# The last batch's second deferred output block: stored at step 14 of chunk 4 in place of step 26 of chunk 3

## The chip, the cores and the metric

One core of a Trainium2 chip runs the program. The metric is the device time of one execution in microseconds (us), lower is better. "Before" is the kernel as it was, "after" the changed one. A trace has its own clock, which starts with the span.

## The reference, cut to what matters

```python
# u, v: (8, 3008, 256); z: (8, 3008, 64); w_in: (256, 2048); w_out: (2048, 256)
scores = (z @ z.T) / 3008                  # batch by batch
x = u * (np.maximum(scores, 0.0) ** 2 @ v)
h = x @ w_in
out = (h / (1 + np.exp(-1.702 * h))) @ w_out
```

The eight batches are independent. The kernel goes through a batch in six chunks of rows (0 to 5), five of 512 and a last one of 448. A score tile is squared on ScalarE and VectorE; because the scores are symmetric, a tile is computed once and its mirror image is made by a transposing DMA into a tile called `tt` (`ad` and `al` are two further kinds of tile that such DMAs fill, for the diagonal and for the last rows).

## The kernel before

The parts that the change and the argument touch. `attend` yields the TensorE steps of one chunk. In each step TensorE multiplies one block of the squared scores with `V`, and other work is slipped in between the steps by their number:

```python
for i in range(NCH):                                  # chunks 0..5
    # ...
    for n, step in enumerate(attend(b, i, b == 0 and i == 0)):
        # ...
        if i == 3 and n in (3, 26) and LAST2:         # <- the line that changes
            LAST2.pop(0)()                            # store one deferred block
        if (i, n) in load:
            load_u(b, load[i, n])
        # ...
        take(host, sched[i].get(n, 0))                # next score tile(s): matmul, square, transpose
        # ...
        step()
```

`LAST2` holds the stores of the last two output blocks of the batch before, put off so that they do not crowd the end of that batch. A store is one 32x32-block transpose on VectorE and then DMAs on SP's queue, four for the block concerned here:

```python
def store(b, k):
    # ...
    yo = pw.tile([P, CH // QW, QW, NCC], F32, name="yo", tag="yo", bufs=1)
    dve.transpose(yo[...], Y[b, k][...])              # cut
    # ...
    for cb in range(P // QW):                         # 4 pieces
        for r, t, n_ in parts:
            sp.dma_start(out[r:r + n_]..., yo[...])   # cut
```

The transposing DMAs of the squared tiles go out on the same queue:

```python
def turn_unit(b, i, jp, a):
    # ...
    sp.dma_start_transpose(TT[b, i, cj][...], a...)   # cut
```

The score pairs of a chunk are made one chunk ahead of their use. In the last batch the fourth tile of chunk 4 is made at step 34 of chunk 3. I call its transpose the **late transpose**; TensorE reads it at step 20 of chunk 4, right after four matmuls on an `ad` tile. The transpose of a `tt` tile issued last before it is its **neighbour**.

## Time and profile before

| | before |
|---|---|
| median of the first three runs | 1180.64 us (1180.33 to 1181.52) |
| profiled execution | 1180.15 us, span 1178.3 us, clock 0.999 |
| TensorE busy | 1171.0 us, 99% of the span |
| VectorE, ScalarE busy | 871.0 us (74%), 849.4 us (72%) |
| share of the DMA engines by queue | SP 52.8%, GpSimd 21.5% |

TensorE is the bound: whatever leaves its idle time alone leaves the time alone. A view of waits names, for an engine, what ended its idle time; a chain of waits follows the last instruction back to what released it. The lines are in the prediction.

### The profile page before, as it was taken

The numbers are of one execution on the slowest core, as the hardware profiler recorded it, in microseconds if no ns is written. First come the engines' busy times: TensorE is split into PE (matmuls) and PEld (weight loads), VectorE is DVE, ScalarE is ACT, GpSimd is POOL, SyncE is SP. The second block draws the span as 40 slices with busy tenths as digits, with TensorE's granted clock in tenths as the row PEclk, the third lists the DMA queues.
The fourth block names the chain that finished last, engine by engine and source line by source line (L and its number), as shares of the span: only waits on it lengthen the run. The fifth ranks groups of instructions, "written<-read, shape, count | busy, mean of one in ns | idle before, by whom it ended". The sixth has DMA issues, their size and how long they took to land.

```text
span 1178.3 us, 23585 instructions
## 1 busy us (share of the span) xinstructions
PE 1171.0 (99%) x9284; PEld 670.0 (57%) x9284; DVE 871.0 (74%) x1455; ACT 849.4 (72%) x1033; POOL 209.4 (18%) x294
## 2 busy tenths in 40 slices
PE   9999999999999999999999999999999999999998
PEld 3546764466644675446754467544674456744566
DVE  7789875878767786587865878658786587764776
ACT  7888874688647886478864787647877578772785
POOL 3033101231012310143101420024100241001000
PEclk9999999999999999999999999999999999999999
DMA  9998679766798677976779568895678955696023
GB/s 223 210 134 129 130 119 158 90 108 135 119 150 94 108 141 127 144 101 93 146 117 154 101 93 149 137 150 88 100 126 142 142 105 94 122 166 120 1 37 73
DMA packets 459039, 143.65 MB, mean 122 GB/s; under 512 B 424624, under 2 KB 453040, under 8 KB 458928
## 3 DMA queue, kind: packets, MB, share of 16 engines
q1 hardware_dynamic: 402464, 102.36, 52.8%
q0 software_dynamic: 55104, 38.49, 21.5%
q8 instruction: 72, 1.18, 0.4%
q10 hardware_dynamic: 1360, 1.31, 0.4%
q14 instruction: 39, 0.32, 0.1%
HBM read 60.29 MB, written 24.64 MB: 72 GB/s over the span
## 4 chain that ended last, share of the span: by engine, by line
PE 98%; ACT 1%; DMA 0%; issue 0%; SPq 0%; DVE 0%
PE o L367 40%; PE hg L408 28%; PE st L532 23%; PE sc L235 6%; PE st L535 1%; PE yp L506 1%; ACT rl L256 0%; DMA tt<-a 0%; PE w L99 0%; ACT W L452 0%; SPq L599 0%; ACT ZT L143 0%; ACT gf L416 0%; PE zp L135 0%; DVE a L270 0%
## 5 line engine op out<-in xcount | busy, mean ns | idle before, releaser
L416 ACT ACTIVATE gf<-hg 128x1024 f32<-128x1024 f32 (+1 forms) x384 | 385.3, 1004 | 114.6 <-PE hg L408 97.7
L256 ACT ACTIVATE rl<-sc 128x1024 f16<-128x1024 f32 (+1 forms) x301 | 287.4, 993 | 143.5 <-PE sc L235 98.4
L367 PEld LDWEIGHTS <-V 64*128 64x128 f16 (+1 forms) x4098 | 219.7, 94 | 252.5 <-issue 9.4
L408 PE MATMUL hg<-xt,W 128*128 128x512 f16 (+1 forms) x1408 | 354.6, 374 | 0.2
L367 PE MATMUL o<-a,V 64*128 64x512 f16 (+3 forms) x2278 | 296.1, 368 | 0.3 <-DVE a L270 0.3
L420 DVE TENSOR_SCALAR gt<-gf 128x1024 f16<-128x1024 f32 (+1 forms) x288 | 200.1, 695 | 114.2 <-ACT gf L416 113.1
L270 DVE TENSOR_TENSOR a<-rl 128x1024 f16<-128x1024 f16 (+1 forms) x266 | 178.1, 674 | 110.4 <-ACT rl L256 109.6
L195 POOL DMA_DIRECT2D uq<-in_u_dram x168 | 111.7, 673 | 739.9 <-PE sc L235 537.1
L367 PE MATMUL o<-tt,V 64*128 64x512 f16 (+1 forms) x1518 | 232.5, 377 | 1.0 <-DMA tt<-a 0.9
L408 PEld LDWEIGHTS <-W 128*128 128x128 f16 x1536 | 149.4, 98 | 125.6 <-issue 2.6
L532 PEld LDWEIGHTS <-WT 128*128 128x128 f16 x1472 | 139.1, 98 | 45.1
L532 PEld LDWEIGHTS <-W 128*128 128x128 f16 x1104 | 104.7, 98 | 32.2
L235 PE MATMUL sc<-ZT 64*128 64x512 f16 (+3 forms) x688 | 115.5, 356 | 0.6 <-ACT ZT L143 0.3
L418 ACT ACTIVATE gt<-gf 128x1024 f16<-128x1024 f32 (+1 forms) x96 | 98.9, 1030 | 3.1
L549 ACT ACTIVATE y<-st 128x256 f32<-128x256 f32 x192 | 70.6, 368 | 35.6 <-PE st L532 29.0
L532 PE MATMUL st<-gt,WT 128*128 128x256 f16 (+1 forms) x736 | 91.9, 268 | 0.0
L532 PE MATMUL st<-s,WT 128*128 128x256 f16 (+1 forms) x736 | 90.8, 268 | 0.0
L532 PE MATMUL st<-gt,W 128*128 128x256 f16 (+1 forms) x736 | 90.8, 268 | 0.0
L553 DVE SCALAR_TENSOR_TENSOR y<-st,y 128x256 f32<-128x256 f32 (+1 forms) x144 | 57.7, 408 | 24.5 <-ACT y L549 11.5
L384 DVE TENSOR_TENSOR xt<-o,ut 128x512 f16<-128x512 f32 x80 | 51.4, 683 | 28.5 <-PE o L367 28.5
L486 DVE TENSOR_TENSOR s<-s,gt 128x1024 f16<-128x1024 f16 (+1 forms) x96 | 65.0, 678 | 1.1
L484 DVE TENSOR_TENSOR s<-gt 128x1024 f16<-128x1024 f16 (+1 forms) x96 | 65.4, 681 | 0.0
(59 smaller groups left out, 670.9 us busy)
## 6 DMA issues: line engine op xcount, KB each, us to landing
out_dram<-yo SPq DMA_DIRECT2D x156, 128.0 KB, 2.8
uq<-in_u_dram POOLq DMA_DIRECT2D x140, 128.0 KB, 3.3
V<-in_v_dram POOLq DMA_DIRECT2D x35, 256.0 KB, 6.1
tt<-a SPq DMA_TRANSPOSE x232, 3.5
uq<-in_u_dram POOLq DMA_DIRECT2D x28, 112.0 KB, 4.7
out_dram<-yo SPq DMA_DIRECT2D x28, 96.0 KB, 6.4
uq<-in_u_dram SPq DMA_DIRECT2D x20, 128.0 KB, 4.3
wst<-in_moe_w_in_dram POOLq DMA_DIRECT2D x4, 512.0 KB, 6.0
```

The lines of the kernel that those rows point to most:

```text
L195: eng.dma_start(uq[k * QW:(k + 1) * QW, :n // QW].rearrange("t q c k -> t q (c k)"), src[:, :, cs])
L235: pe.matmul(sc[:, r, :q1 - q0], zt[h, 2 * kp + r, :], zt[h].rearrange("d n p -> d (n p)")[:, q0:q1], start=True, stop=True,)
L256: act.activation(rl[:, :, :n], sc[:, :, :n], AF.Relu, scale=csc)
L270: dve.tensor_tensor(a[:, :, :n], rl[:, :, :n], rl[:, :, :n], ALU.mult)
L367: ins = pe.matmul(acc[c][:, :n], V16[b][h, j].rearrange("p (c k) -> p k c", k=NCC)[:, c], weights(b, i, j)[h], start=(k, m) == first[c], s ...
L408: pe.matmul(hg[:, e, :n], W1[:, c, ff * P:(ff + 1) * P], XT[b, i][:, c, :n], start=(c == 0), stop=(c == NCC - 1),)
L416: act.activation(gf[:, :, :n], hg[:, :, :n], AF.Gelu_apprx_sigmoid, scale=1.0 / FSC)
L418: act.activation(g, gf[:, :, :n], AF.Copy, scale=FSC)
L420: dve.tensor_scalar(g, gf[:, :, :n], FSC, None, ALU.mult)
L484: dve.tensor_tensor(s_, a21, a22, ALU.add)
L532: pe.matmul(bank, right[:, ff], lhs()[:, f], start=first, stop=last, skip_group_check=True)
L549: act.activation(y[:, c, :, o], bank, AF.Copy, scale=1.0 / FSC)
```

## The change

The intent is to get the second deferred store of the last batch out of the way of the transposes issued late in chunk 3. `more` is true for all batches but the last, so the other batches keep their order.

```diff
-                if i == 3 and n in (3, 26) and LAST2:
+                if (i, n) in ((3, 3), (3, 26) if more else (4, 14)) and LAST2:
                     LAST2.pop(0)()
```

## The prediction

> **What bounds the kernel now.** I read the page first (busy shares, slices, the chain that ended last), then the waits of TensorE, then the chain and the timeline of the only place that the diff touches, which is the last of eight batches. The page:
>
> ```profile
> PE 1171.0 (99%) x9284; PEld 670.0 (57%) x9284; DVE 871.0 (74%) x1455; ACT 849.4 (72%) x1033; POOL 209.4 (18%) x294
> PE   9999999999999999999999999999999999999998
> PE 98%; ACT 1%; DMA 0%; issue 0%; SPq 0%; DVE 0%
> ```
>
> TensorE is busy 1171.0 of 1178.3 us, and the chain lies on it for 98% of the span. So only TensorE's own idle time can be won here, 7.3 us in all, most of it at the start and after the last matmul. Who TensorE waited for, over the whole span:
>
> ```profile
> PE w L99 <- DVE nil L75: 1.2, 1, 1.2
> PE o L367 <- DMA tt<-a: 0.9, 1, 0.9
> PE o L367 <- DVE a L270: 0.3, 1, 0.3
> ```
>
> In the middle of the kernel a single named wait is worth anything: 0.9 us, once, on a transposing DMA. The waits of the other kind of TensorE instruction, the weight loads, show the same event as 1.4 us, once, because the loads run ahead of the matmuls. The chain between 1072 and 1081 us shows what it was, with a view cut to that window:
>
> ```profile
> 1072.23 0.93 ACT rl L256
> ...
> 1073.18 0.63 DVE a L270
> 1073.80 0.14 DVE a L273
> 1073.95 0.07 SPq L599
> ...
> 1074.07 0.57 SPq L599
> ...
> 1075.24 0.47 SPq L599
> ...
> 1075.83 4.57 DMA tt<-a
> 1080.39 0.04 issue
> 1080.44 1.04 PE o L367 x8
> ```
>
> Read it backwards. Matmuls at 1080.44 waited for the transpose, which took 4.57 us from issue to landing. Its input was ready at 1073.94, but the DMA queue of SP was then issuing the four pieces of the second deferred output block (line 599), and only at 1075.83 did it come to the transpose. That block is the one that the diff moves. The timelines of SP and TensorE:
>
> ```profile
> 1071.92 1.23 SPq L298 DMA_TRANSPOSE tt<-a  x1
> 1073.24 2.47 SPq L599 DMA_DIRECT2D out_dram<-yo  x4
> 1075.83 1.25 SPq L298 DMA_TRANSPOSE tt<-a  x1
> 1077.44 2.98 SPq L277 DMA_TRANSPOSE al<-a  x2
> ```
>
> ```profile
> 1078.90 0.59 PE L367 MATMUL o<-ad,V 64*128 64x512 f16 x4
> 1080.44 1.04 PE L367 MATMUL o<-tt,V 64*128 64x512 f16 x8 [0.94 <-DMA tt<-a]
> ```
>
> **What the Trainium skill says.** "DMA: Bandwidth & Descriptors", section "Anatomy of one DMA — SWDGE (gpsimd) path", says that any semaphore wait happens on the issuing sequencer before dispatch; so an instruction behind another one on SP waits for it. The trace agrees: 1.89 us pass between input ready (1073.94) and issue (1075.83), filled by line 599. The same page, section "Queues, rings and completion order", says that each DMA engine consumes one row's descriptors in ring order, so the transpose also stands behind the stores' 384 KB as data. The trace agrees in kind: the transpose issued at 1071.92 ahead of the stores and the one at 1075.83 behind them are both among the slow ones, 4.7 and 4.57 us to landing, where the median of all 232 is 3.5. "Perfetto Trace Analysis", section "Summary: the profiler window per engine type", says that the window of such a DMA leaves out the data movement; hence I use the times to landing (4.57), not the 1.25 us of the timeline row.
>
> **The change, part by part.** Nothing is added or removed. For the last batch, one store moves from step 26 of chunk 3 to step 14 of chunk 4. The instruction lists of the two programs differ so: TensorE, ScalarE and GpSimd keep their order; on VectorE the layout transpose of the block (128x768, 0.97 us at 1071.81) moves behind the squares of three score tiles and the two gates; on SP the four stores move behind the late transpose and behind the two al transposes.
>
> *Removed on the path.* The late transpose is issued when its input is ready. Its producer does not get earlier: ScalarE's row at 1072.23 waits for the score matmul at 1071.83, so VectorE is done at 1073.94 as before. With 0.08 us to issue (1073.95 to 1074.02 in the chain) it goes out at about 1074.0. Landing: median 3.5 gives 1077.5; the slow 4.7 of its neighbour gives 1078.7. TensorE's weight loads need it when the loads before it end, 1075.26 + 3.74 = 1079.0, and the matmuls at 1078.90 + 0.59 = 1079.5. So it lands 0.3 to 1.5 us early for the loads and 0.8 to 2.0 us early for the matmuls. The whole 0.94 us goes.
>
> *Moved on VectorE.* The 0.97 us now falls at about 1077.4, after the square that ends at 1077.37. VectorE then has nothing until 1082.17 (the profile shows 4.81 us of idle there), so it costs nothing.
>
> *Moved on SP.* The four stores go out after the al transposes, from about 1080.4, taking 2.5 us; landing 2.8 more, so about 1086. SP's next own DMA is a store past 1125 us. On GpSimd's queue the last load of u (issued from 1082.27) shares the DMA engines with them; it is used by VectorE at 1092.45, over 5 us after it would land even if it took twice its 2.8 us. The al transposes are used by matmuls at 1086.57, and land by about 1082.4 as before or sooner.
>
> *Does the gain reach the end?* From 1081 to 1087 us TensorE is busy 5.97 of 6.00, and then 23.00 of 23.00 and 55.00 of 55.00 us up to 1165; the chain from there on is matmuls, one VectorE add and the last store. No other engine holds TensorE there, so everything shifts forward by the same amount. Sum: -0.94 + 0 + 0 = -0.94 us, 1180.64 - 0.94 = 1179.7 us, a change of 0.08%.
>
> **Rivals.** (1) *The wait shrinks but stays.* The transpose still shares the engines with the u load that GpSimd issued at 1070.34 to 1072.92 and stands behind the transpose of 1071.92. For: that neighbour took 4.7 us, and the slowest of all took 10.2. Against: without 384 KB of stores between the two, the queue has little left when the neighbour lands at 1076.6, and back-to-back transposes are issued 1.3 us apart elsewhere and land 3.2 to 3.8 us after issue. A landing of 6 us would leave 0.5 us of the wait: 1180.2 us. (2) *The stores do harm in their new place*, by delaying the u load of the last chunk or the al transposes. For: VectorE needs that load for its gate of chunk 5. Against: 5 us of slack or more for each, and SP issues the al pair first. Were there 1 us of delay, the time would be 1180.7, as before. (3) *Removing a wait uncovers another*: a score tile or gate not ready 0.94 us sooner. For: TensorE would reach chunk 5 sooner. Against: no other named TensorE wait exists past 1081 us, and the gates, scores and first up-products are themselves triggered by TensorE and shift with it. A new hitch would be 0.3 us or less: 1180.0. (4) *The gain is real but not visible in the medians*, as the three runs of before lie 1.19 us apart (1180.33 to 1181.52), more than the gain itself.
>
> **Range and chances.** I give 75% to the full gain, 15% to a part of it, 10% to nothing or to a small loss. All of these lie within 1 us; the spread of three runs and of chips adds about as much. So 1179.7 us, 1178.8 to 1180.8 in 8 of 10 cases. A 2% change would be 23.6 us, 25 times the only wait that is touched: within 2% is as good as certain, 0.98, with 0.01 on either side for a disturbed run.
>
> **What would show each step right or wrong.** In the profile of the changed kernel: the wait of the matmuls of o on tt is missing from TensorE's list; the transpose of tt of chunk 4 goes out at about 1074.0, right after the one of 1071.92, and lands by 1078.7; SP's four stores of the 96 KB kind stand behind the al pair near 1080.4; TensorE is busy 2.00 of the 2.00 us from 1079 to 1081; the span falls from 1178.3 to about 1177.4. I would be wrong if that transpose landed after 1079.5, if a new wait of TensorE past 1081 us appeared (on u's layout transpose or on al), or if the span fell by clearly more than 0.94 us, which would mean that idle time which I took for unconnected was hanging on it.

## More of the kernel before

Products of `x` with `w_in` are made in what the kernel calls up-groups.

One more line of the page matters later. It is from the list of DMA queues, with packets, megabytes and share of 16 engines' span:

```profile
q8 instruction: 72, 1.18, 0.4%
```

These are 72 packets, 1.18 MB together and some 16 KB each, on a queue of its own.

## The result, and the profile after

| | before | after |
|---|---|---|
| median | 1180.49 us (6 runs, 1180.13 to 1183.37) | 1179.29 us (6 runs, 1179.20 to 1179.84) |
| profiled span | 1178.3 us | 1177.7 us |
| TensorE's wait on `tt` | 0.9 us, once | none |

A ratio here is the mean time of one kernel's runs over the mean of the other's in the same rounds, so it is not quite the ratio of the medians quoted. It is 0.9986, with a 95% interval of 0.9973 to 0.9999: the same within 2%, and in the predicted range of 1178.8 to 1180.8 us.

The page of after, by busy time and by the engines of the chain that ended last:

```profile
PE 1171.1 (99%) x9284; PEld 670.1 (57%) x9284; DVE 870.9 (74%) x1455; ACT 849.7 (72%) x1033; POOL 208.0 (18%) x294
PE 99%; ACT 1%; DVE 0%; issue 0%
```

The work is that of before; the DMA and SP entries have left the chain. TensorE's waits in after, whole list (total us, times, longest):

```profile
PE w L99 <- DVE nil L75: 1.2, 1, 1.2
PE o L367 <- DVE a L270: 0.3, 1, 0.3
PE sc L235 <- ACT ZT L143: 0.3, 1, 0.3
PE zp L135 <- DVE zst L128: 0.2, 1, 0.2
PE sc L235 <- ACT rl L256: 0.2, 1, 0.2
```

The wait on `tt` is gone, and those that are left all fall in the first 15 us. SP's queue in after, as a timeline (start, us, instruction):

```profile
1072.42 3.28 SPq L298 DMA_TRANSPOSE tt<-a  x2
1077.93 2.69 SPq L277 DMA_TRANSPOSE al<-a  x2
1080.74 2.08 SPq L599 DMA_DIRECT2D out_dram<-yo  x4
```

The neighbour and the late transpose now go out one behind the other, the second at 1074.47, which is 0.03 us after its input is ready (VectorE ends at 1074.44). The DMA view of after, cut to the tenth of a microsecond in which the late transpose is issued (count, us to landing):

```profile
tt<-a SPq DMA_TRANSPOSE x1, 3.3
```

It lands at about 1077.8, 3.3 us after its issue. In before it took 4.57 us, from an issue 1.89 us after the input was ready. TensorE in after:

```profile
1079.40 0.59 PE L367 MATMUL o<-ad,V 64*128 64x512 f16 x4
1079.84 1.03 PE L367 MATMUL o<-tt,V 64*128 64x512 f16 x8
```

The transpose is there 2.0 us before its first matmul (1079.84 - 1077.8); these 2.0 us are its slack.

**The stall cost 1.10 us, not the 0.94 us that the profile prints as idle.** From the start of the four `ad` matmuls to the start of the first `tt` matmul it is 1080.44 - 1078.90 = 1.54 us before and 1079.84 - 1079.40 = 0.44 us after. The difference is 1.10. The printed idle time begins at the modelled end of the last `ad` matmul, and that end lies 0.16 us later than the next matmul would have started. The Trainium skill says in "Perfetto Trace Analysis", section "Tensor Engine Instruction (MATMUL, LD_WEIGHTS)", that this end is estimated; here the effect has a size.

**The spans differ by only 0.6 us because the profiled run of after lost 0.5 us at its start.** A TensorE line of the first 10 us, before:

```profile
8.56 0.39 PE L135 MATMUL zp<-ident,zst 128*128 128x128 f16 x4
```

and after:

```profile
9.05 0.40 PE L135 MATMUL zp<-ident,zst 128*128 128x128 f16 x4 [0.23 <-DVE zst L128]
```

The diff does not reach the first batch. The 0.49 us stays: the matmul on `sc` that begins chunk 4 starts at 1075.26 before and at 1075.76 after. Taking it off, 1.10 - 0.50 = 0.60, the difference of the spans.

### The profile page after: what moved, and what is told of

Same layout as the page of the kernel before. It is cut to its first block, busy times and chain, and to the rows that moved or that the text cites. A ratio compares the mean times of both kernels' runs of the same rounds, so it can differ in the third digit from the quotient of the medians.

```text
span 1177.7 us, 23588 instructions
## 1 busy us (share of the span) xinstructions
PE 1171.1 (99%) x9284; PEld 670.1 (57%) x9284; DVE 870.9 (74%) x1455; ACT 849.7 (72%) x1033; POOL 208.0 (18%) x294
## 4 chain that ended last, share of the span: by engine, by line
PE 99%; ACT 1%; DVE 0%; issue 0%
PE o L367 40%; PE hg L408 28%; PE st L532 23%; PE sc L235 6%; PE st L535 1%; PE yp L506 1%; PE w L99 0%; ACT rl L256 0%; ACT W L452 0%; ACT gf L416 0%; PE zp L135 0%; ACT ZT L143 0%; DVE a L270 0%; DVE zst L128 0%; DVE y L553 0%
```

## The experiments

The changed kernel once more and eleven variants ran, five times or more each, beside runs of before on the same chip. A microsecond is less than 0.1% of the time, and single executions of one kernel lie over 5 us apart at the most, so the traces carry the verdicts and the medians only support them: by their ratios all twelve are the same within 2%, and only the interval of e3 (1.0011 to 1.0035) lies clear of 1. A trace is one execution of its kernel. Other executions may lose more or less: single runs of e8 and e13 took 1179.34 and 1179.40 us, as little as the changed kernel. In the table, "lost" is the time from the start of the last `ad` matmul to that of the first `tt` matmul, less the 0.21 us that it takes in every trace without a wait; before has 1.11 us by this count. "Flight" is issue to landing of the late transpose.

| run | what is ahead of or beside the late transpose | flight, us | lost, us | median less that of before, us |
|---|---|---|---|---|
| (before) | 4 stores ahead on SP | 4.57 | 1.11 | |
| a0_after | nothing | 4.06 | 0 | 1179.69 - 1180.77 = -1.08 |
| e1_turn_stays | nothing (VectorE as before) | 3.44 | 0 | 1179.29 - 1180.77 = -1.48 |
| e2_gpsimd_queue | 4 stores beside it, GpSimd's queue | 7.06 | 1.74 | 1181.38 - 1180.77 = +0.61 |
| e3_eight_pieces | 8 half stores ahead on SP | 3.21 | 3.07 | 1183.06 - 1180.77 = +2.29 |
| e8_act_queue | 4 stores beside it, ScalarE's queue | 7.32 | 2.00 | 1180.97 - 1180.56 = +0.41 |
| e6_after_square | nothing; 4 stores right behind on SP | 3.37 | 0 | 1179.53 - 1180.56 = -1.03 |
| e9_twelfth_bytes | 4 stores of 8 KB ahead on SP | 4.88 | 1.07 | 1180.38 - 1180.56 = -0.18 |
| e4_three_stay | 3 stores ahead on SP | 4.78 | 0.80 | 1181.19 - 1180.56 = +0.63 |
| e10_before_96_more | 4 stores ahead on SP | 3.35 | 0.59 | 1180.56 - 1180.72 = -0.16 |
| e12_before_256_more | 4 stores ahead on SP | 4.59 | 1.13 | 1181.68 - 1180.72 = +0.96 |
| e11_after_32_more | nothing | 5.04 | 0 | 1179.61 - 1180.72 = -1.11 |
| e13_before_200_more | 4 stores ahead on SP | 4.53 | 1.32 | 1180.07 - 1180.58 = -0.51 |

One sum ties the rows together. In after, an unhindered first `tt` matmul starts 5.40 us after the transpose's input is ready (1079.84 - 1074.44), and some 0.05 us pass between landing and matmul. So what is lost is the lateness of the issue plus the flight less 5.35 us: 1.89 + 4.57 - 5.35 = 1.11 before, 5.22 + 3.21 - 5.35 = 3.08 in e3 (issue at 1079.75, input ready at 1074.53), and the other rows come out within 0.03 us. With the flight of after, 3.34 us, the late issue of before would have lost nothing (1.89 + 3.34 = 5.23): by this sum the stall of before needed both the late issue and the longer flight. No run has exactly this pair, so it is worked out, not shown.

The theory: the four stores, issued on SP ahead of the late transpose, make it late. The rivals: VectorE's moved transpose is what counts; the data in the DMA engines is, not SP's issue; and, later, something else on the DMA engines.

### The changed kernel again (a0_after)

No edit. 

> The changed kernel once more, paired with the kernel before. If the stall costs what the first matmuls of the late transpose lose from start to start (16.46 us before and 15.36 us after, from the first matmul of chunk 3 to the first matmul that needs the transpose), it is 1.1 us faster; if it costs only the idle time that the profile prints (0.94 us), 0.94 us. No TensorE wait on tt in the trace. The start of the kernel (first 10 us) differs by up to half a microsecond between runs of either kernel, which says nothing of the change.

The late transpose took 4.06 us and still landed 1.3 us early (1083.41, first use 1084.72): no wait on `tt`. The median is 1.08 us lower, but the ratio is 0.9996 (0.9983 to 1.0009), because one of six runs took 1184.43 us. That run is the profiled one, and its trace says why: in the first batch VectorE's layout transpose of `u` waited 4.7 us for its load, and TensorE then stood still for 3.3 us at 66 us, in code that the change does not touch.

### VectorE's part undone (e1_turn_stays)

```diff
         for cb in range(P // QW):
+            if b == B - 2 and k == NCH - 1:                # shortened: `piece` is the sp.dma_start of one piece
+                OFF.append(lambda cb=cb: piece(cb, sp))
+                continue
# ... and in the loop over the steps, the pop at (3, 26) kept as it was:
+                if (i, n) == (4, 14):
+                    while OFF:
+                        OFF.pop(0)()
```

> Only the four DMA stores move to chunk 4, the block's 0.97 us layout transpose on VectorE stays at step 26 of chunk 3. If SP's queue is the cause: no TensorE wait on tt, the late transpose is issued 0.1 us after its input is ready, time as the changed kernel (1.1 us below before). If VectorE's place in the order is the cause: the wait of 0.9 us stays and the time is that of before.

There is no wait on `tt`, and the median is 1.48 us below before. Only SP's part of the change is needed; in this trace VectorE's part is worth nothing.

### The stores on another queue (e2_gpsimd_queue, e8_act_queue)

```diff
-                OFF.append(lambda cb=cb: piece(cb, sp))      # of the kernel above, run at (4, 14)
+                OFF.append(lambda cb=cb: piece(cb, pool))    # e2: run at (3, 45); e8: act, run at (3, 35)
```

> The four stores of the block keep their time (about 1073 to 1076 us) but are issued by GpSimd after its u load, so SP is free and the data still shares the 16 DMA engines. If the delay is SP's issue alone: the late transpose goes out at about 1074.0 and lands within 3.5 us, no TensorE wait, 1.1 us below before. If the 384 KB of data are the cause: it goes out at 1074.0 but lands 5.5 us or more later, and a wait of 0.3 us or more stays.

> As the GpSimd experiment, but the four stores are issued by ScalarE's queue right after the late square (about 1073.2 us), where ScalarE has 2.5 us without work. SP is free, the 384 KB cross the DMA engines at the old time on another ring. If any data in flight beside the transpose delays it: issued at about 1074.0, landing after 5.3 us or more, a TensorE wait of 0.2 us or more stays. If the 7.06 us of the GpSimd experiment were special to GpSimd's queue: it lands within 4.5 us, no wait on tt, 1.1 us below before.

SP was free and issued the late transpose as soon as its input was ready; it landed later than before all the same. The chain of waits of the GpSimd kernel:

```profile
1073.80 0.15 DVE a L273
1073.95 0.02 issue
1073.97 7.06 DMA tt<-a
1081.03 0.05 issue
1081.08 1.04 PE o L367 x8
```

and of the ScalarE kernel:

```profile
1074.41 7.32 DMA tt<-a
```

The neighbour was slowed as well, from 4.7 to 6.0 and 6.3 us. So SP's issue time is not the only thing that can cause the stall: the transpose flew longer with the stores on another queue beside it than with the same stores ahead of it in its own (7.06 and 7.32 against 4.57 us). A packet on the queue q8 was in flight with the late transpose in all three (the section on the instruction fetch says what it is), but it began only at 1078.99 in e2 and 1079.56 in e8, when the transpose had flown 5.0 and 5.2 us already, so it is not the whole of it. In e8 it may be the last part: fifteen of the sixteen landing events had come by 1080.43, the sixteenth at 1081.73. The Trainium skill, "DMA: Bandwidth & Descriptors", section "Issuing engines are not separate DMA queues", says that DMAs from all issuing engines share the 16 DMA engines and interleave; the longer flights fit that, and show the cost. Why it is this large I did not find out.

### The stores right behind the late transpose (e6_after_square)

```diff
-                if i == 3 and n in (3, 26) and LAST2:
+                if (i, n) in ((3, 3), (3, 26) if more else (3, 36)) and LAST2:
```

> The second block is stored at step 36 of chunk 3, directly behind the late transpose on SP: only the order of two neighbours on SP is swapped against before, the bytes are in flight almost at the same time. If the order in the SP ring is what counts: the transpose lands within 3.5 us of 1074.0, no TensorE wait on tt, 1.1 us below before. If bytes in flight at that time delay it whatever the order: it lands after 5.3 us or more and a wait stays.

SP's queue:

```profile
1073.87 3.28 SPq L298 DMA_TRANSPOSE tt<-a  x2
1077.24 2.21 SPq L599 DMA_DIRECT2D out_dram<-yo  x4
```

The flight is 3.37 us, nothing is lost, and the median is 1.03 us below before. The whole gain comes from putting the late transpose ahead of the four stores; moving them a further 25 steps on is not needed. (Its profiled run, 1180.99 us, again had a hitch in the first batch, a 2.0 us wait of TensorE on ScalarE's cast of the weights.)

### More issue time, the same bytes (e3_eight_pieces)

```diff
+        if b == B - 2 and k == NCH - 1:
+            parts = [(r0, 0, n // 2), (r0 + n // 2, n // 2, n // 2)]
```

> As before, but in the last batch this block is stored in eight pieces of half the size: the same bytes, about twice the issue time on SP (some 4 us in place of 2.5). If SP's issue sets the end of the wait: the transpose goes out about 1.5 to 2 us later and TensorE's wait grows from 0.94 us by as much, so 1.5 to 2 us slower than before. If the data does: the landing stays at about 1080.4 us and the time is that of before.

SP was busy with the eight pieces for 5.50 us in place of 2.47, and 3.07 us were lost, 1.96 more than before; the median rose by 2.29 us. The transpose that goes out behind all 384 KB flies only 3.21 us. Time on SP ahead of the transpose therefore reaches the end of the kernel once the slack is gone.

### The same issue, almost no bytes (e9_twelfth_bytes)

Its output is wrong, which doesn't matter for the time. Each store writes 32 of 384 rows.

```diff
+        if b == B - 2 and k == NCH - 1:
+            parts = [(r0, 0, QW)]
```

> Wrong on purpose: the four stores stay at step 26 of chunk 3 on SP, but each writes only the first 32 of 384 rows (8 KB in place of 96), so most of that block of the output is not written. SP's issue time stays (about 2 us), the data is all but gone. If issue alone is enough for the stall: a TensorE wait near 0.9 us stays. If issue and data together are needed (1.8 us of issue delay against 2.0 us of slack): the transpose goes out near 1075.5 and lands 3.3 us later at about 1078.8, no wait, 1.1 us below before.

I had leant to the second of these, and it fell. SP's queue:

```profile
1073.31 2.11 SPq L601 DMA_DIRECT2D out_dram<-yo  x4
1075.54 1.24 SPq L298 DMA_TRANSPOSE tt<-a  x1
```

and the step of the chain of waits that follows:

```profile
1075.54 4.88 DMA tt<-a
```

32 KB in place of 384 KB ahead of it, and the late transpose still flew 4.88 us, and 1.07 us were lost. So it is not the bytes of the stores that make the flight of before 1.2 us longer than that of after. e3 above, and e10 below (3.35 us), say the same from the other side: behind all the bytes the flight can be as short as in after.

### A quarter of the stores moved (e4_three_stay)

```diff
-            if b == B - 2 and k == NCH - 1:                # of e1_turn_stays: put off to (4, 14)
+            if b == B - 2 and k == NCH - 1 and cb >= 3:    # the fourth piece alone
```

> Three of the four stores stay at step 26 of chunk 3, one moves to step 14 of chunk 4. The transpose goes out 0.57 us earlier than before (about 1075.25) behind 288 KB in place of 384, and lands some 0.9 us earlier, at about 1079.4, against a need at 1079.34: a wait of 0 to 0.3 us, so nearly the whole gain, 0.8 to 1.1 us below before. If the gain came in proportion to the stores moved, it would be a quarter, 0.3 us, and a wait of 0.7 us would stay.

The issue came 0.5 us earlier against the input than before (1.37 us late, not 1.89), as expected, but the flight of 4.78 us ate it up: 0.80 us were lost, close to the proportional rival's 0.7. The trace's landing events tell more. It has sixteen for this transpose. Fifteen had come by 1079.93, a flight of 3.2 us and early enough to lose nothing; the sixteenth came at 1081.50. In the packet records, a packet of 16 KB on the queue q8 had begun at 1079.51 and taken 0.96 us.

### Moving the instruction fetch (e10, e12, e11, e13)

That queue is the fetch of TensorE's program. The Trainium skill, "Runtime: NRT & Kernel Launch", section "Instruction fetch mechanics", says that an engine's instructions are fetched in blocks of 16 KiB (256 instructions) by a DMA queue of the sequencer. The trace agrees: 9284 matmuls and as many weight loads, 18568 instructions, make 72.5 such blocks against 72 packets, and between two of these packets lie 256 traced TensorE instructions on average. In before one began at 1077.56, took 1.17 us, and 21 packets of the transposes beside it took 1.27 to 1.62 us in place of some 0.02. In after the fetch began at 1078.06, just after the late transpose had landed.

More rows in TensorE's program shift the place of the fetch. Some up-groups of batch 5 compute 512 columns as twice 256, with the same results and next to no time:

```diff
+                if b == 5 and 8 <= q < 8 + GROUPS:   # 12, 32, 4, 25 groups: 96, 256, 32, 200 rows
+                    for m in range(2):
+                        x = slice(m * CH // 2, (m + 1) * CH // 2)
+                        pe.matmul(hg[:, e, x], W1[...], XT[b, i][:, c, x], ...)
+                    continue
```

> The kernel before, stores where they were; in batch 5 twelve up-groups compute each 512 columns as two of 256, which adds 96 rows to TensorE's program and next to no time. TensorE's program is fetched in pieces of 16 KB, one for each 256 rows, and one such fetch (1077.56 us before, 1.17 us on one DMA engine) met the late transpose. The rows move that fetch some 5 us earlier. If the fetch is needed for the stall: the transpose still goes out 1.9 us late behind the stores, but lands 3.2 to 3.4 us later, before it is needed: no wait on tt, about 1.0 us below before (less what the extra matmuls cost, at most 0.5 us). If the stores ahead of it suffice: landing after 4.5 us and a wait near 0.9 us as before.

> Control for the last one: 32 up-groups split, 256 more rows, so a whole fetch more and the fetches stand where they stood against the late transpose. If the fetch is needed for the stall: the wait on tt is back (0.5 to 1.2 us). If the extra rows themselves took the wait away: no wait on tt.

> The changed kernel with 32 more rows in TensorE's program, so that the fetch comes about 1.7 us earlier, while the late transpose moves its data (it landed 0.25 us before the fetch in the first profile of the changed kernel). If a fetch delays a transpose: it lands 4 to 5 us after issue in place of 3.3; with 2.0 us of slack before it is needed, still no wait on tt, and the time of the changed kernel. If the fetch does nothing: landing 3.3 us as before.

> The experiment with 96 rows moved the fetch onto the transpose before, which held up SP. With 200 more rows (25 groups split) and the stores still where the kernel before has them, one fetch should come some 11 us before the old place and the next about 3 us after it, 1080.6 us on the clock of before, clear of both transposes. If the fetch is needed for the stall: the late transpose goes out 1.9 us after its input is ready, lands 3.3 us later (1079.1 on the clock of before, need 1079.34), wait 0 to 0.1 us. If the stores ahead of it suffice: the wait of 0.9 us is back.

With 96 rows the fetch came about 5 us earlier on before's clock, as intended, and the late transpose flew 3.35 us. But 0.59 us were still lost: the fetch now met the neighbour, which flew 5.72 us and held SP for 2.32 us in place of 1.23, so the late transpose went out later. With 256 rows, a whole block, the fetch was back on the late transpose, and so were the flight of 4.59 us and 1.13 us lost. With 32 rows in the changed kernel the fetch fell on both transposes. The DMA view of that run at the issue of the late one:

```profile
tt<-a SPq DMA_TRANSPOSE x1, 5.0
```

It landed at 1079.00, 0.34 us before its first matmul at 1079.34: 1.7 of the 2.0 us of slack were used up and nothing was lost. So far the fetch explains the longer flights on SP's queue: 4.06 to 5.04 us in the six traces in which it was in flight with the late transpose for 0.7 us or more (before, a0, e4, e9, e11, e12), 3.21 to 3.44 in the other five (after, e1, e3, e6, e10).

The 200 rows put an end to the simple story. No fetch of TensorE's program was near (1067.18 and 1083.42), yet the chain of waits shows

```profile
1076.54 4.53 DMA tt<-a
1081.07 0.05 issue
1081.12 1.04 PE o L367 x8
```

and 1.32 us were lost. This time GpSimd's load of `u` was slow (its last piece took 6.4 us, 4.4 before), the neighbour beside it flew 6.96 us, the issue of the late transpose itself took SP 2.46 us in place of 1.25, and everything behind came late. What made all of them slow is open. A fetch is one thing that can take up the slack; it is not the only one. Nor is the place special: in e4 and e12 TensorE also waited 0.6 and 1.2 us, near 75 us in the first batch, for another `tt` transpose, which flew 5.2 and 6.2 us with no fetch of TensorE's program beside it.

Over the whole trace of before, the 56 of 232 transposes that had a fetch in flight between 1.5 us after issue and landing took 4.57 us (median), the other 176 took 3.33. That favours the fetch, but a longer flight also meets a fetch more easily, so it is no proof.

## Why the prediction was right

- **The bound and the only wait.** Right. The wait on `tt` is gone, no other replaced it past the start, and the profile after keeps TensorE busy 55.00 of 55.00 us from 1110 to 1165, as before. (From 1079 to 1081 it is 1.97 of 2.00, where 2.00 was forecast.)
- **Removed on the path: issued at 1074.0, landing 1077.5 to 1078.7.** Right. The profiled run of after is 0.50 us late from its start on; on the clock of before, the transpose was issued at 1073.97 and landed at 1077.3. That the order on SP is enough is shown by e1 and e6: with none of the four DMA stores ahead of it on SP, nothing is lost, in five of five traces (after, a0, e1, e6, e11). With stores ahead on SP, or beside it on another queue, something is lost in nine of nine, before included. What the prediction did not see is that, by the sum above, the 1.89 us of late issue alone would not have stalled TensorE: they fit into the 2.0 us of slack, and only with the flight of 4.57 us in place of 3.34 did they cost 1.1 us.
- **Moved on VectorE, free.** Right: at 1077.78 for 0.97 us, and e1, which leaves it where it was, gains as much.
- **Moved on SP, free.** Right. The stores went out at 1080.74 and the last landed at 1085.8. The load of `u` issued beside them took 3.4 to 3.9 us a piece, 2.6 to 2.9 before; the last piece landed at 1087.05 and was used at 1091.84. The al pair landed by 1081.8. Two readings were loose, without consequence. The 2.8 us to landing is the page's median for stores of 128 KB; for 96 KB the page has 6.4 us, and these four took 2.1 to 3.5. And the slack of "over 5 us" for `u` holds at the old 2.8 us; at twice that, with the last piece issued at 1084.14, it is 2.7.
- **The sum of -0.94 us.** The mechanism was right and the size was too small by about a seventh: the term is 1.10 us from start to start, as the printed idle of TensorE leaves out 0.16 us. The medians moved by 1.20 us at first, and by 1.03 to 1.48 us in the four further runs without the wait. These differences carry run-to-run noise of the same order.
- **"The transpose also stands behind the stores' 384 KB as data."** Not borne out: with a twelfth of the bytes its flight was no shorter (e9), and behind all of them it was 3.21 and 3.35 us (e3, e10). The reading offered for it could not carry it either, since the transpose ahead of the stores was as slow (4.7 us) as the one behind them. The prediction did not need this step, since it took the landing from the transposes of the trace.
- **Rival 1, a slow landing**, is what came nearest to spoiling the gain. In e11 the flight was 5.04 us, and the slack of 2.0 us just covered it. That after's first profile met no fetch in flight, by 0.25 us, was luck; that the gain came was not, since a0 and e11 met one and lost nothing. The "3.2 to 3.8 us" for transposes issued 1.3 us apart was too narrow: of the 104 in before that were issued within 1.4 us of the one ahead, a quarter took over 4.2 us and the slowest 10.2. Rival 2's delay of the load was there, 0.8 to 1.1 us a piece, and stayed within its slack. Rival 3 was not seen. Rival 4 held: the repeat's ratio of 0.9996 (0.9983 to 1.0009) cannot tell the gain from nothing, while the traces can.

What stays open: why all the DMAs around the late transpose were slow in e13, without a fetch, and why it flew 7 us beside stores on a second queue. Nothing tried beats the changed kernel by more than the noise; e1 and e6 equal it.

## What to carry to other kernels

When an in-order DMA queue carries both transfers that the bounding engine waits for and transfers that nobody waits for, issue the first kind first: swapping the transpose and the stores was worth the whole gain here, and handing the stores to another queue lost more in the traces. Do the sum of lateness and flight against the slack before calling one of them the cause. Judge the size of a TensorE stall from start to start against an undisturbed stretch, not by the printed idle time. And when the gain is 0.1%, decide by what is gone from the trace, because the medians alone cannot.

## What the Trainium skill lacked or had wrong

- "DMA: Bandwidth & Descriptors" says that DMAs on several queues interleave, but not what this does to a transpose: with four 96 KB stores on GpSimd's or ScalarE's queue beside it, it took 7.06 and 7.32 us to land, with the same stores ahead of it on its own queue 4.57 (all three with a fetch of TensorE's program in flight, too), and 3.3 without either.
- "Runtime: NRT & Kernel Launch" calls the fetch of a 16 KiB block mostly hidden, and no page says what it does to other DMAs. For TensorE itself these runs show no wait put down to it, but its packet took about 1 us (median over 72 packets), and in one trace fifteen of a transpose's sixteen landing events had come by 1079.93 and the sixteenth only at 1081.50, with a fetch begun at 1079.51.
- "Perfetto Trace Analysis" says that a matmul's end is an estimate; no page says how much idle time this hides. Here it is 0.16 us for the gap behind the 64x512 matmuls (0.94 printed, 1.10 from start to start), and 0.17 by the count of "lost" in each of the nine traces that have the gap.
